# Attention and two MLPs on one core: input loads before weights, merged value sums, masks as matmuls, filler matmuls, a later third attention

## The chip, the cores and the metric

One core of a Trainium2 chip runs the whole program in one launch. The metric is the device time of an execution in microseconds (us); the time of a kernel is the median of its runs. The engines are PE (matmuls; PEld is its weight load), DVE (vector), ACT (scalar, activations), POOL (GpSimd) and SP, whose queue issues the loads and stores.

## What is computed

Four batches of eight heads, 576 positions, 64 channels; two attentions are added, and two MLPs follow on all 2304 tokens. From the reference, shortened:

```python
q_d = q.reshape(B, H, Sd, factor, D).mean(axis=3)     # factor 4, k and v alike
out_d = sm_attn(q_d, k_d, v_d)
out_up = np.repeat(out_d, factor, axis=2)
mask = np.abs(pos[:, None] - pos[None, :]) < factor
scores = np.where(mask, scale * np.matmul(q, k.transpose(0, 1, 3, 2)), -1000000000.0)
...
x = out_up + out_local                                 # 2304 x 512
h = x @ w_in
y = (h * np.cos(h)) @ moe_w_out                        # 512 -> 2048 -> 512
z = ((y @ w_a) * (y @ w_b)) @ moe2_w_out               # 512 -> 1536 -> 512
```

All of it is float32.

## The kernel before

The tokens are worked on in eight half-batches of 288 (`u` = 0 to 7; even `u` is the first half of a batch). Attention goes by pairs of heads (`hp` = 0 to 3). For each pair: `down_sums` adds groups of four keys (`kd`) and queries (`qd`), line L180 on DVE or L182 to L184 on POOL; `local_scores` multiplies five windows of 64 keys (L207, 10 matmuls of 64x64 that the profile shows as 20), adds the band mask on DVE (L218), takes the row maximum (L222) and subtracts it (L223); `down_scores` does the pooled scores (L234 to L237). Exponentials, normalisation, transposes through PE (L300, L309), the products with the values (L319, L326) and `combine` follow. `sum_vs` adds the four parts of the pooled values on POOL (L173 to L175). `xsplit_hi` and `xsplit_lo` split the result into a rounded high part (`xh`) and a low rest (`xl`).

Every weight chunk (128x512, 8 bytes an element as it lies in memory) is loaded (`wload`, L102) and made into a high and a low half by five instructions: L111 on ACT, L112 and L113 on DVE, L115 on ACT, L116 on POOL. There are 32 of them for the first MLP. A product is three matmuls (`mm3`, L429 to L431): high times high, high times low, low times high.

The first half-batch is done by itself (the prologue: lines 516 to 556). Then a loop over steps `g` runs one `h_mm` (12 matmuls into a PSUM tile `h`), the cosine (L475, L476, L480, L483, L484), the split of the result (L488, L492) and, three steps later, `back_mm` (12 matmuls into four `acc` tiles). Blocks 0 and 1 are the first two half-batches with the first 8 of 16 chunks, whose results go to `y_part`; half-batch 2 enters at step 32. The attention of the next half-batches is spread over the steps by `unit_slots(u, g0, gl)`: it begins at step `g0` and takes `gl` steps, by the table `C['T']`. For half-batch 2 that is `unit_slots(2, C["G2"], 2 * NF - C["G2"])`, from step 14 to 32.

The code is traced by a scheduler (Tile), which sets each engine's fixed order from its own estimates; each engine then runs its order and waits for semaphores. Loads and stores stand in SP's queue in order. PSUM has eight banks: `att` 2, `h` 2, `acc0` to `acc3`; in the prologue `att_ps` also takes those of `h` and `acc`. `vs` has one buffer for `u` > 0, `q` three, and the tiles of stores (`ev`) share three with `xf`.

Of the kernel before, what the change touches and what calls it, by code (L numbers as in the profile page):

```python
# [40 lines left out]
C = {'AHEAD': 8, 'LEAD': 4, 'NPRE': 4, 'ND': 'ddd', 'XL': 'dpp', 'SUMS0': 'dddd', 'SUMS1': 'pppp', 'GLO': 8, 'FS': 8, 'S1': 0.7, 'G2': 14, 'LC': 0, 'DM': 2, 'LAG': 3, 'NGS': 3, 'MK': 0, 'SB': 'ddd', 'NL': 'dpp', 'W0': 0, 'W1': 0, 'W2': 0, 'W3': 0, 'NWV': 3, 'NGH': 4, 'XB': 8, 'YE': 6, 'CA': 2, 'NR': 3, 'PA': 1, 'LAG2': 2, 'PK': 1.0, 'GE': 'ad', 'NXF': 3, 'LP': 0, 'T': {'sums': [0, 0.5, 1.0, 3.0], 'ls': [0, 0, 0, 1.5], 'ds': [1, 1.5, 3, 4], 'ex': 6, 'ln': [6.0, 9.5], 'dn': [6, 7, 9, 10], 'dt': [7, 9.5, 11, 12], 'lt': [7.5, 8.5, 12.0, 13.5], 'at': [9.5, 9.5, 13.5, 14.5], 'xh': [11.0, 12.0, 15.0, 15.5], 'xl': [12.5, 13.5, 15.5, 15.5]}, 'T1': {'sums': [0, 0, 1.0, 2.0], 'ls': [0.5, 1.5, 2.5, 3.5], 'ds': [1, 1.5, 3, 4], 'ex': 5, 'ln': [5.5, 8], 'dn': [5.0, 6.0, 8.0, 9.0], 'dt': [6.0, 7.5, 10.0, 11.0], 'lt': [7.0, 8.0, 12.0, 12.0], 'at': [9, 9, 13, 14], 'xh': [9.0, 10.0, 13.0, 14.0], 'xl': [9.5, 11, 15, 15]}}  # L41
# [16 lines left out]
def kernel(ctx, tc, qT, kT, vw, vds, w_in, w_out, w_a, w_b, w_out2, out):  # L58
# [96 lines left out]
    def load_vs(u, hp, par):  # L155
        b, half = divmod(u, 2)
        if half == 0:
            if u == 0:
                t = wp.tile([QD, 2, 4, D], F32, tag="w", name="vs0", bufs=33)
            else:  # L160
                t = at.tile([QD, 2, 4, D], F32, tag="vs", name="vs", bufs=1)
            ins = sp.dma_start(out=t, in_=vds[b, 2 * hp + par])
            after(ins, gate.get(u))
            vst[u, hp, par] = t

    def sum_vs(u, hp, par):
        b, half = divmod(u, 2)
        if half == 0:
            t = vst.pop((u, hp, par))
            if par == 0:  # L170
                vdt[b, hp] = at.tile([QD, 2, 2, D], F32, tag="vd", name="vd", bufs=4)
            o = vdt[b, hp][:, par]
# [25 lines left out]
    def local_scores(u, hp):  # L198
# [5 lines left out]
        for w, (off, _, _, _) in enumerate(window_cols(half)):  # L204
            for a in range(2):
# [5 lines left out]
                    start=not pem, stop=True,  # L211
# [293 lines left out]
    if C["MK"]:  # L505
        identb = const.tile([128, 128], BF16, name="identb")
        maskb = const.tile([128, W], BF16, name="maskb")
        pool.tensor_copy(out=identb, in_=ident)
        pool.tensor_copy(out=maskb, in_=mask)

    if C["W0"]:
        first.remove("acc3")
        wz = at.tile([128, 128], BF16, name="wz")
        dve.memset(wz, 0.0)
        wps = [ps.tile([128, 4, 128], F32, tag="acc3", name="wps")]
# [191 lines left out]
```

## Time and profile before

| | |
|---|---|
| median of three runs | 1035.38 us (1032.7, 1035.38, 1037.63) |
| the profiled execution | 1032.1 us, of which 1030.3 from its first to its last instruction (span) |
| busy: PE, PEld, DVE, ACT, POOL | 990.4, 901.4, 526.0, 470.0, 185.7 us |
| loads and stores | 72.70 MB, mean 71 GB/s |

PE's busy share counts matmuls that overlap one another; equal matmuls stand at two paces in this trace (rows 3), so a stretch with a full PE need not be PE at its fastest. A group's mean is over all its places; where a row gives the idle time before it and what ended it, that is a wait as the profile infers it. In a timeline "x12" means that twelve neighbours were merged, and the time is that from the first one's start to the last one's end.

### The profile page before, as it was taken

To read this page: it belongs to the slowest core of one execution; us is meant where nothing else is said; L and a number is where in the kernel's file an instruction comes from. 1 tells how busy PE (TensorE), PEld (TensorE's weight loads), DVE (VectorE), ACT (ScalarE), POOL (GpSimd) and SP (SyncE) were. 2 spreads that over 40 slices of the span, in tenths; PEclk is the share of its full clock that TensorE was granted. 3 is DMA by queue.
4 is the path that set the end of the run, shared out by engine and by line. 5 is a ranking of instruction groups with operands and counts; after the bars stand their busy time and mean duration, and the time that the engine had idled before them with its cause. 6 is when DMAs were issued, how large, how long until landed. Compare 5 with 4: busy or idle time off the path is not lost.

```text
span 1030.3 us, 16803 instructions
## 1 busy us (share of the span) xinstructions
PE 990.4 (96%) x6720; PEld 901.4 (87%) x6720; DVE 526.0 (51%) x1076; ACT 470.0 (46%) x1018; POOL 185.7 (18%) x215
## 2 busy tenths in 40 slices
PE   5978799999999899999999999999999999999998
PEld 4768799998989799899999988898898899889987
DVE  7889975676667465563687883121122113112111
ACT  4687676474747375564777653121122112111111
POOL 4878731012101300000232441000000001000000
PEclk9989999999999899999999999999999999999999
DMA  9645311312120201000443760020021002001000
GB/s 303 216 160 212 113 52 38 89 42 62 48 84 21 82 13 33 24 1 8 162 148 122 226 194 28 1 74 1 1 65 40 1 1 83 1 1 37 1 1 37
DMA packets 35021, 72.70 MB, mean 71 GB/s; under 512 B 5504, under 2 KB 19840, under 8 KB 34944
## 3 DMA queue, kind: packets, MB, share of 16 engines
q1 hardware_dynamic: 34944, 71.65, 21.8%
q8 instruction: 52, 0.85, 0.4%
q14 instruction: 25, 0.20, 0.1%
HBM read 61.01 MB, written 10.62 MB: 70 GB/s over the span
## 4 chain that ended last, share of the span: by engine, by line
PE 73%; issue 7%; POOL 7%; DVE 6%; DMA 5%; ACT 3%; SPq 0%; POOLq 0%; DVEq 0%
PE acc L429 9%; PE acc L430 9%; PE acc L431 9%; PE h L429 5%; PE h L431 5%; PE h L430 5%; PE pb L431 4%; PE pa L430 4%; PE pb L429 4%; PE pa L431 4%; PE pa L429 4%; PE pb L430 4%; POOL w L116 3%; DVE raw L113 2%; DMA vs<-in_vds_dram 2%
## 5 line engine op out<-in xcount | busy, mean ns | idle before, releaser
L429 PE MATMUL acc<-gh,w 128*128 128x288 f32 (+3 forms) x648 | 220.7, 341 | 1.1 <-DVE ev L468 1.1
L430 PE MATMUL acc<-gl,w 128*128 128x288 f32 (+3 forms) x648 | 217.5, 336 | 1.7 <-POOL gl L492 1.7
L431 PE MATMUL acc<-gh,w 128*128 128x288 f32 (+3 forms) x648 | 216.0, 333 | 0.0
L647 DVE TENSOR_TENSOR gs<-gs,pb 128x460 f32<-128x460 f32 (+1 forms) x60 | 38.0, 633 | 267.6 <-PE pb L431 267.5
L488 ACT ACTIVATE gh<-gs 128x288 fp32r<-128x288 f32 (+3 forms) x172 | 88.6, 515 | 161.8 <-DVE gs L647 119.2
L429 PE MATMUL h<-xh,w 128*128 128x288 f32 (+1 forms) x448 | 145.7, 325 | 6.0 <-DVE gs L484 6.0
L431 PE MATMUL h<-xh,w 128*128 128x288 f32 (+1 forms) x448 | 141.8, 317 | 1.7 <-POOL w L116 1.7
L430 PE MATMUL h<-xl,w 128*128 128x288 f32 (+1 forms) x448 | 141.7, 316 | 0.0
L492 DVE TENSOR_TENSOR gl<-gs,gh 128x288 fp32r<-128x288 f32 (+3 forms) x164 | 105.4, 643 | 62.1 <-ACT gh L488 60.9
L429 PEld LDWEIGHTS acc<-gh,w 128*128 128x128 f32 x648 | 122.9, 190 | 11.2 <-issue 3.5
L430 PEld LDWEIGHTS acc<-gl,w 128*128 128x128 f32 x648 | 123.1, 190 | 8.5 <-POOL gl L492 1.9
L431 PEld LDWEIGHTS acc<-gh,w 128*128 128x128 f32 x648 | 123.0, 190 | 5.8 <-issue 0.4
L644 ACT COPY gs<-pa 128x460 f32<-128x460 f32 (+1 forms) x60 | 32.5, 541 | 179.6 <-PE pa L431 179.6
L116 POOL TENSOR_TENSOR w<-raw,w 128x512 fp32r<-128x512 f32 x62 | 85.9, 1393 | 71.0 <-ACT w L115 70.9
L429 PEld LDWEIGHTS h<-xh,w 128*128 128x128 f32 x448 | 85.5, 191 | 11.8 <-DVE gs L484 8.9
L431 PEld LDWEIGHTS h<-xh,w 128*128 128x128 f32 x448 | 85.5, 191 | 3.5 <-POOL w L116 2.3
L430 PEld LDWEIGHTS h<-xl,w 128*128 128x128 f32 x448 | 85.5, 191 | 1.5 <-issue 0.6
L475 ACT ACTIVATE gs<-h 128x288 int32<-128x288 f32 (+1 forms) x112 | 49.5, 442 | 68.6 <-PE h L431 68.4
L476 DVE SCALAR_TENSOR_TENSOR gs<-gs,h 128x288 f32<-128x288 int32 (+1 forms) x112 | 55.1, 492 | 39.1 <-ACT gs L475 38.6
L429 PE MATMUL pa<-xh,w 128*128 128x460 f32 (+1 forms) x200 | 73.8, 369 | 1.1 <-ACT gs L644 1.1
L431 PE MATMUL pb<-xh,w 128*128 128x460 f32 (+1 forms) x200 | 74.4, 372 | 0.0
L430 PE MATMUL pa<-xl,w 128*128 128x460 f32 (+1 forms) x200 | 74.4, 372 | 0.0
(100 smaller groups left out, 1683.6 us busy)
## 6 DMA issues: line engine op xcount, KB each, us to landing
raw<-in_w_out_dram SPq DMA_DIRECT2D x28, 512.0 KB
raw<-in_w_in_dram SPq DMA_DIRECT2D x16, 512.0 KB
raw<-in_w_a_dram SPq DMA_DIRECT2D x12, 512.0 KB
raw<-in_w_b_dram SPq DMA_DIRECT2D x12, 512.0 KB
v<-in_vw_dram SPq DMA_DIRECT2D x16, 320.0 KB
q<-in_qT_dram SPq DMA_DIRECT2D x32, 146.0 KB
k<-in_kT_dram SPq DMA_DIRECT2D x16, 288.0 KB
vs<-in_vds_dram SPq DMA_DIRECT2D x32, 144.0 KB
```

The costliest lines, as they stand in the source:

```text
L113: ins = dve.scalar_tensor_tensor(out=lw, in0=hh, scalar=3, in1=lw, op0=ALU.logical_shift_left, op1=ALU.bitwise_or)
L116: lo_eng.tensor_tensor(out=t[:, 1], in0=lw.bitcast(F32), in1=t[:, 0].bitcast(F32), op=ALU.subtract)
L429: i = pe.matmul(ps_out, lh, rh, start=start, stop=False)
L430: pe.matmul(ps_out, lh, rl, start=False, stop=False)
L431: pe.matmul(ps_out, ll, rh, start=False, stop=stop)
L475: act.activation(out=k, in_=hps[g], func=AF.Copy, scale=1.0 / (2.0 * math.pi))
L476: dve.scalar_tensor_tensor(out=gs[g], in0=k, scalar=-2.0 * math.pi, in1=hps[g], op0=ALU.mult, op1=ALU.add)
L488: act.activation(out=gh[g], in_=gs[g], func=AF.Copy)
L492: eng.tensor_tensor(out=gl[g], in0=gs.pop(g), in1=gh[g].bitcast(F32), op=ALU.subtract)
L644: act.copy(out=gs[g], in_=pa)
L647: dve.tensor_tensor(out=gs[g], in0=gs[g], in1=pb, op=ALU.mult)
```

## The change

- The prologue's loads: SP issues the four `k` first and ACT's queue the four `q`; then one weight chunk, two `vs`, a weight, and values and `vs` by turns; the other weights last.
- For the first half-batch, the pooled values of a pair come by one load of 72x1024 in place of two of 72x512, and three adds of 72x256 replace six of 72x128. The layout of `vds` in memory is changed to suit.
- Pairs 2 and 3 of the first half-batch form `kd` and `qd` on POOL (`SUMS0` 'ddpp').
- For half-batches 0, 1 and 2 (`MK` 3) the mask is added by PE: a bf16 matmul of the identity with the mask, into the tile that the scores are then added to. The bf16 operands are the upper halves of the float32 identity and mask. DVE takes the maximum from PSUM and subtracts from PSUM.
- Filler matmuls of 128x512 in bf16, whose result nobody reads: 4 before the first scores, 3 after each of the four pairs' scores, 10 before the first transposes. They take the `acc3` bank in the prologue and are kept in program order.
- `local_scores` is written ahead of `down_sums` in the prologue.
- The third attention (half-batch 2) begins at step 18 in place of 14 (`G2`).

Its core as a diff:

```diff
-C = {... 'SUMS0': 'dddd', ... 'G2': 14, ... 'MK': 0, ... 'W0': 0, 'W1': 0, 'W2': 0, 'W3': 0, ...}
+C = {... 'SUMS0': 'ddpp', ... 'G2': 18, ... 'MK': 3, ... 'W0': 4, 'W1': 3, 'W2': 10, ...}
-                t = wp.tile([QD, 2, 4, D], F32, tag="w", name="vs0", bufs=33)
+                t = wp.tile([QD, 4, 4, D], F32, tag="w", name="vs0", bufs=33)
+                sp.dma_start(out=t, in_=vds[b, hp])
-            o = vdt[b, hp][:, par]
+            o = vdt[b, hp] if u == 0 else vdt[b, hp][:, 2 * par:2 * par + 2]
-                    start=not pem, stop=True,
+                    start=not pem, stop=not pem or w == NW - 1,
-                pe.matmul(wps[0], wz, wz.unsqueeze(1).to_broadcast([128, 4, 128]), start=True, stop=True)
+                tc.keep_in_program_order(pe.matmul(wps, identb, identb.unsqueeze(1).to_broadcast([128, 4, 128]), start=True, stop=True))
+    identb, maskb = (t.bitcast(BF16).rearrange("p (c t) -> p t c", t=2)[:, 1] for t in (ident, mask))
         for hp in range(HP):
             load_k(0, hp)
-            load_q(0, hp)
-            if hp < C["NPRE"]:
-                load_next(None)
-        for hp in range(HP):
-            for par in range(2):
-                load_vs(0, hp, par)
-        load_v(0)
-        for _ in range(C["AHEAD"] - C["NPRE"]):
+            load_q(0, hp, act)
+        load_next(None)
+        load_vs(0, 0, 0)
+        load_vs(0, 1, 0)
+        load_next(None)
+        load_v(0, 0)
+        load_vs(0, 2, 0)
+        load_vs(0, 3, 0)
+        load_v(0, 1)
+        for _ in range(C["AHEAD"] - 2):
             load_next(None)
         warm(C["W0"])
         for hp in range(HP):
+            local_scores(0, hp)
             down_sums(0, hp)
-            local_scores(0, hp)
             warm(C["W1"])
...
         down_exp(0, 3)
+        warm(C["W2"])
         for hp in range(HP):
-            for par in range(2):
-                sum_vs(0, hp, par)
+            sum_vs(0, hp, 0)
```

What the scheduler makes of it. PE's order at the start of the program, before (`att` is a score tile, `wps` the fillers' tile):

```order
L207 MATMUL att<-k,q 64x64 x10
L234 MATMUL att<-kd,qd 72x144
L207 MATMUL att<-k,q 64x64 x10
L234 MATMUL att<-kd,qd 72x144 x3
L207 MATMUL att<-k,q 64x64 x10
```

and now, where the numbers show which pair it is (`kd_183` and `qd_185` are pair 1, `k_97` and `q_99` pair 0):

```order
L235 MATMUL att_237<-kd_183,qd_185 72x144
L235 MATMUL att_238<-kd_183,qd_185 72x144
L390 LDWEIGHTS ident_75
L390 MATMUL wps_96<-ident_75 128x512
...
L390 MATMUL wps_96<-ident_75 128x512
L204 LDWEIGHTS ident_75
L204 MATMUL att_145<-mask_76,ident_75 128x320
L208 MATMUL att_145<-k_97,q_99 64x64 x10
```

PE's first matmuls are now the pooled scores of pair 1; four fillers and the mask stand ahead of the first local scores.

DVE's order at the start, before:

```order
L180 TENSOR_REDUCE kd<-k 128x144
L180 TENSOR_REDUCE qd<-q 128x72
L236 TENSOR_REDUCE mxd<-att 72x1
L112 TENSOR_SCALAR raw<-raw 128x512
L180 TENSOR_REDUCE kd<-k 128x144
L180 TENSOR_REDUCE qd<-q 128x72
L113 SCALAR_TENSOR_TENSOR raw<-raw 128x512
```

and now:

```order
L181 TENSOR_REDUCE qd<-q 128x72
L181 TENSOR_REDUCE kd<-k 128x144
L181 TENSOR_REDUCE qd<-q 128x72
L181 TENSOR_REDUCE kd<-k 128x144
L112 TENSOR_SCALAR raw<-raw 128x512
L113 SCALAR_TENSOR_TENSOR raw<-raw 128x512
L223 TENSOR_REDUCE mx<-att 128x5
L224 TENSOR_TENSOR smx<-att,mx 128x5x64
```

The sums of pairs 0 and 1 stand together, and the first weight's two instructions stand ahead of the first row maximum.

SP's order around the third attention, before (`vs` are the pooled values of half-batch 2, `y_part` the stores of a block's result):

```order
L162 DMA vs<-in_vds_dram 72x512 x2
L143 DMA q<-in_qT_dram 128x292 x2
L162 DMA vs<-in_vds_dram 72x512 x2
L143 DMA q<-in_qT_dram 128x292
L162 DMA vs<-in_vds_dram 72x512 x2
L143 DMA q<-in_qT_dram 128x292
L162 DMA vs<-in_vds_dram 72x512
L470 DMA y_part<-ev 128x288 x4
```

and now:

```order
L102 DMA raw<-in_w_out_dram 128x512
L163 DMA vs<-in_vds_dram 72x512 x6
L143 DMA q<-in_qT_dram 128x292 x2
L471 DMA y_part<-ev 128x288 x4
L143 DMA q<-in_qT_dram 128x292 x2
```

Six `vs` loads in a row now stand ahead of the `q` loads.

## Rows read from the trace of the kernel before

**Rows 1.** Table of stretches: length, busy PE, PEld, DVE, ACT, POOL, PE clock, DMA.

```profile
3.68:36.77 33.09, 24.74 (x244) 19.74 (x244) 27.03 (x67) 17.55 (x51) 19.32 (x29) 1.00 0.87 303
36.77:118.23 81.46, 66.23 (x584) 58.26 (x583) 74.83 (x134) 63.42 (x152) 65.57 (x59) 0.92 0.55 183
118.23:160.00 41.77, 38.89 (x305) 36.48 (x306) 33.68 (x82) 28.90 (x66) 17.49 (x22) 0.96 0.15 43
160.00:220.00 60.00, 60.00 (x586) 56.44 (x585) 37.43 (x95) 36.54 (x89) 3.22 (x4) 1.00 0.20 62
0.00:34.42 34.42, 22.39 (x235) 17.39 (x235) 24.69 (x62) 16.97 (x48) 18.80 (x37) 1.00 0.89 306
```

**Rows 2.** Chain of waits of the prologue: start us, us, what.

```profile
7.78 7.67 DMA vs<-in_vds_dram
...
31.99 0.45 POOL vd L175
```

**Rows 3.** Timeline of PE and its weight loads around the first `h`: start, us.

```profile
34.42 0.61 PE L429 MATMUL h<-xh,w 128*128 128x288 f32 x1
34.58 0.33 PEld L430 LDWEIGHTS h<-xl,w 128*128 128x128 f32 x1
...
37.23 0.44 PE L431 MATMUL h<-xh,w 128*128 128x288 f32 x1
...
40.77 0.29 PE L429 MATMUL h<-xh,w 128*128 128x288 f32 x1
...
41.43 0.29 PE L431 MATMUL h<-xh,w 128*128 128x288 f32 x1
```

**Rows 4.** Timeline of DVE, the fifteenth `h`.

```profile
118.23 0.45 DVE L476 SCALAR_TENSOR_TENSOR gs<-gs,h 128x288 f32<-128x288 int32 x1 [0.51 <-ACT gs L475]
```

**Rows 5.** DVE's groups by shape, 0 to 140 us: busy us, mean ns, idle before.

```profile
L223 DVE TENSOR_TENSOR smx<-smx,mx 128x320 f32<-128x320 f32 x12 | 8.0, 681 | 0.0
L180 DVE TENSOR_REDUCE kd<-k 128x144 f32<-128x576 f32 x8 | 5.9, 742 | 4.0 <-DMA k<-in_kT_dram 4.0
L218 DVE TENSOR_TENSOR smx<-att,mask 128x320 f32<-128x320 f32 x12 | 5.6, 479 | 0.6 <-PE att L207 0.6
L180 DVE TENSOR_REDUCE qd<-q 128x72 f32<-128x288 f32 x9 | 4.0, 439 | 0.0
```

**Rows 6.** The same for 0 to 36.77 us.

```profile
L223 DVE TENSOR_TENSOR smx<-smx,mx 128x320 f32<-128x320 f32 x4 | 1.8, 480 | 0.0
```

**Rows 7.** POOL's groups by shape, 2.4 to 34.15 us.

```profile
L175 POOL TENSOR_TENSOR vd<-vd,vs 72x128 f32<-72x128 f32 x8 | 6.4, 801 | 0.6
L173 POOL TENSOR_TENSOR vd<-vs 72x128 f32<-72x128 f32 x8 | 5.6, 704 | 13.2 <-DMA vs<-in_vds_dram 13.2
L174 POOL TENSOR_TENSOR vd<-vd,vs 72x128 f32<-72x128 f32 x8 | 3.8, 476 | 0.6
L116 POOL TENSOR_TENSOR w<-raw,w 128x512 fp32r<-128x512 f32 x1 | 1.3, 1302 | 0.4 <-ACT w L115 0.4
```

**Rows 8.** Timeline of DVE and ACT, the first two weights.

```profile
6.62 0.43 DVE L112 TENSOR_SCALAR raw<-raw 128x512 uint32<-128x512 uint32 x1
...
9.08 0.66 ACT L111 ACTIVATE raw<-raw 128x512 f32<-128x512 f32 x1 [1.29 <-DMA raw<-in_w_in_dram]
```

**Rows 9.** Timeline of PE at the third attention's first scores.

```profile
120.04 1.33 PE L207 MATMUL att<-k,q 64*64 64x64 f32 x20 [2.58 <-DVE smx L218]
...
121.71 0.44 PE L430 MATMUL acc<-gl,w 128*128 128x288 f32 x1
121.95 0.44 PE L431 MATMUL acc<-gh,w 128*128 128x288 f32 x1
```

**Rows 10.** Chain of waits, 340 to 358 us.

```profile
341.52 2.36 DMA vs<-in_vds_dram
...
345.95 4.12 DMA y_dram<-ev
```

**Rows 11.** Timeline of PE, 347 to 355 us.

```profile
350.71 0.80 PE L207 MATMUL att<-k,q 64*64 64x64 f32 x20 [2.04 <-DVE xf L338]
...
354.25 1.33 PE L207 MATMUL att<-k,q 64*64 64x64 f32 x20 [2.41 <-DVE smx L218]
```

More of the change, by code (lines that the diff above doesn't have):

```diff
@@ L134, in load_k, with load_q @@
             kt[b, hp] = t
-    def load_q(u, hp):
+    def load_q(u, hp, eng=sp):
         if u < NU:
@@ L142, in load_q, with load_v @@
                 t = at.tile([128, HALF], F32, tag="q", name="q", bufs=3)
-            sp.dma_start(out=t, in_=qT[b, hp, :, BASE[half]:BASE[half] + HALF])
+            eng.dma_start(out=t, in_=qT[b, hp, :, BASE[half]:BASE[half] + HALF])
             qt[u, hp] = t
-    def load_v(u):
-        for pr in range(HP // 2 if u < NU else 0):
+    def load_v(u, *prs):
+        for pr in (prs or range(HP // 2)) if u < NU else ():
             if u == 0:
@@ L158, in load_vs @@
             if u == 0:
-                t = wp.tile([QD, 2, 4, D], F32, tag="w", name="vs0", bufs=33)
+                t = wp.tile([QD, 4, 4, D], F32, tag="w", name="vs0", bufs=33)
+                sp.dma_start(out=t, in_=vds[b, hp])
             else:
                 t = at.tile([QD, 2, 4, D], F32, tag="vs", name="vs", bufs=1)
-            ins = sp.dma_start(out=t, in_=vds[b, 2 * hp + par])
-            after(ins, gate.get(u))
+                ins = sp.dma_start(out=t, in_=vds[b, hp, :, 2 * par:2 * par + 2])
+                after(ins, gate.get(u))
             vst[u, hp, par] = t
@@ L170, in sum_vs @@
             if par == 0:
[L171 to L172 removed]
+                vdt[b, hp] = at.tile([QD, 4, D], F32, tag="vd", name="vd", bufs=4)
+            o = vdt[b, hp] if u == 0 else vdt[b, hp][:, 2 * par:2 * par + 2]
             pool.tensor_tensor(out=o, in0=t[:, :, 0], in1=t[:, :, 1], op=ALU.add)
@@ L319, in attend @@
                 pe.matmul(
-                    p[64 * a:64 * a + 64, NB:NB + QD], vdt[b, hp][:, a, c], pd[u, hp][:, 2 * a + c],
+                    p[64 * a:64 * a + 64, NB:NB + QD], vdt[b, hp][:, 2 * a + c], pd[u, hp][:, 2 * a + c],
                     start=(c == 0), stop=(c == 1),
@@ L503 @@
                            fill=-8e9, base=3, channel_multiplier=-1)
[L505 to L515, printed above, removed]
+    identb, maskb = (t.bitcast(BF16).rearrange("p (c t) -> p t c", t=2)[:, 1] for t in (ident, mask))
+    first.remove("acc3")
+    wps = ps.tile([128, 4, 128], F32, tag="acc3", name="wps")
     if True:
@@ L676, in _layout @@
                 vw[u, hp // 2, hp % 2, :, w] = v[b, 2 * hp:2 * hp + 2, s0:s0 + W].transpose(1, 0, 2)
-    vds = v.reshape(B, H, 2, QD, 4, D).transpose(0, 1, 3, 2, 4, 5)
+    vds = v.reshape(B, HP, 2, 2, QD, 4, D).transpose(0, 1, 4, 2, 3, 5, 6).reshape(B, HP, QD, 4, 4, D)
     return {
```

4 lines of the change are left out of this document (1 added, 3 removed).

## The prediction

> **What bounds the kernel now.** The page comes first, but its shares of busy time are averages over stages. The table of stretches says where PE is not full [rows 1]. From 160 us PE is busy 60.00 of 60.00, and there the diff changes nothing but an address. Before 160 us three stretches differ. From 3.68 us, where DVE gets its first input, to 36.77, where DVE writes the last low half of the first half-batch, DVE is busy 27.03 of 33.09 us and PE 24.74. From there to 118.23, DVE is busy 74.83 of 81.46 and PE 66.23. From 118.23 to 160, PE is busy 38.89 of 41.77 and DVE only 33.68. So up to 118 us the engine nearest to full is DVE, after it PE. The chain of waits names another engine for the prologue: the 24 adds of `sum_vs` on POOL, which start when the first `vs` lands at 15.45 and end at 32.44 [rows 2], with the first weight's low half behind them and the first `h` matmul at 34.42 [rows 3]. Both readings hold: POOL ended last, and DVE had only 6.06 us to spare. That decides the size of my number, because the change takes much from POOL and little from DVE.
>
> **The change, part by part.** I count up to 118.23 us on DVE, where the fifteenth `h` is reduced (L476, the fifteenth of its line, [rows 4]), and after it on PE.
>
> *Masks as matmuls.* Twelve L218 adds go, 479 ns each [rows 5]. Eight of them stand before 118.23: 8 x 0.479 = 3.8 us off DVE. The last four, of the third half-batch, lie where DVE has slack and count nothing here. PE gets twelve matmuls of 320 columns. No row shows one in bf16; twelve of 288 columns start within 2.81 us in the first `h` group, 0.24 apart after the first, and 0.13 apart later [rows 3], so 0.15 to 0.27 each. Eight lie beside DVE's work while PE is idle for 8 and 15 us of the two stretches: nothing. Four lie where PE is full: up to 1.1 us, and I take 0.6. If the cover goes, all twelve cost 3.2.
>
> *The subtraction reads PSUM.* L223 has both inputs in SBUF and takes 480 ns in the prologue (4 of them) and 681 on average over twelve, so (12 x 681 - 4 x 480) / 8 = 782 for the other eight [rows 5, 6]. L218, which reads PSUM, stays at 479 in all. The new subtraction has L218's kind of input, and I price it like L218: 0.30 us off each of the four in the second half-batch, 1.2 us (between 0 and 1.2). The Trainium skill's "SBUF — State Buffer", section "Who interferes with whom", gives a reason: a DVE instruction with two SBUF inputs contends with a GpSimd instruction that reads SBUF, one with a single SBUF input does not; by it the whole 1.2 comes. Its "Perfetto Trace Analysis", section "Optimizing Scalar/DVE Operations", speaks against the edit, with about 125 ns of access overhead on PSUM against 60 on SBUF; an estimate from that page is 16 reads x 65 ns = 1.0 us more, and the sum would be 7.4 in place of 8.4. The rows do not show that: 479 with a PSUM input, 480 without.
>
> *Pooled sums.* The `kd` and `qd` reductions of pairs 2 and 3 leave DVE: 2 x (0.742 + 0.439) = 2.4 us [rows 5].
>
> *POOL.* The 24 adds of 72x128 took 5.6, 3.8 and 6.4 us by line, 15.8 together [rows 7]. Twelve of 72x256 replace them. The nearest rows are 72x128 at its shortest, 0.45 [rows 2], and 128x512 at 1.30 (L116, rows 7); four times the width costs 0.85 more, so 256 costs some 0.73: 8.8 us in all. Twelve small adds for `kd` and `qd` come to POOL, about 0.5 each by L174's 476 ns: 6 us. POOL can start them when pairs 2 and 3 land, near 8.7, not at 15.6, and is done by some 25 us. POOL no longer ends the prologue. DVE's instructions with two SBUF inputs meet as many POOL adds as before.
>
> *Loads.* Keys and weights of before shared one queue. The tiles hold 288 (`k`), 146 (`q`), 512 (a weight) and 144 KB (`vs`). In their old order 946 KB are in at 6.62 us, when DVE starts on the first weight, 1892 at 9.08, when ACT starts on the second [rows 8], and 3928 at 15.45 [rows 2]. Now the four pairs (1736 KB) are first: by the same rate they are in at 8.7, and the first weight, at 2248 KB, at 10.2 instead of 6.62. ACT issues the four `q` loads before its first work, which needs PE's first scores: nothing. DVE's queue is now both sums of pairs 0 and 1, then the first weight's two instructions, and only then the first row maximum. So DVE works some 2.4 us on the sums, waits for pair 1 (about 2 us) and for the weight until 10.2 (about 2), then for ACT's 0.66 us in between [rows 8]: near 5 us idle by 11.6. The waits that follow (local scores behind fillers, the last `qd` from POOL, the attends) I put at 3. DVE idles 8 in place of 6.06: 2.0 us lost. The bounds are 5 (a gain of 1) and 10 (a loss of 4). On that path DVE's last low half of the first half-batch comes at 3.7 + 24.3 + 8 = 36 us, hardly earlier than 36.77; 24.3 is 27.03 less 4.3 (four masks, 2.4 of sums), plus 1.6 for one weight chunk and one maximum that now stand ahead of it.
>
> *Fillers.* 26 matmuls of 512 columns cost 26 x 0.24 = 6.1 us at the later rate and 26 x 0.43 = 11.1 at the first. The column of the granted clock reads 1.00 in the prologue, but the first `h` group stands 0.24 apart, the rate of the lower of the two levels (1.2 GHz), after a prologue in which PE paused often; 0.13 is reached only after 40 us [rows 3]. With fillers the attention of the prologue and the first group may run at 2.4 GHz. I count neither gain nor cost, since DVE covers it: PE had 12 us idle before 34.42 [rows 1].
>
> *Third attention later.* Its scores now start after the last weight has been split on DVE. Of the 41.77 us after 118.23 PE loses 2.88 idle [rows 1], and some 1.1 to slow matmuls after the 2.58 us wait at 117.4 (six `acc` at 0.24, the first of them in [rows 9], and twenty L207 in 1.33 instead of 0.80, [rows 9, 11]). The third of the new `L208` groups can still wait for a PSUM buffer. I take 4.0 less 0.4 for that and less the 0.6 of masks: 3.0, between 0 and 4.
>
> **Sum:** 3.8 + 1.2 + 2.4 - 2.0 + 3.0 = 8.4 us less. The profiled execution took 1032.1 (span 1030.3 and 1.8 around it), so 1023.7; the median of the three runs stands 3.3 above it, and for a median I forecast **1027.0**. With both ends of every unknown it is 1021 to 1034.
>
> **Rivals.**
> 1. *POOL alone ended the prologue.* If DVE's waits in the new order are as short as before or shorter, the first `h` matmul comes with POOL's end plus one L116, near 27 us, 7.4 earlier, and twelve matmuls at 0.13 for 0.24 give 1.3: 8.7 in place of the prologue's share of my sum (1.9 + 2.4 - 2.0 = 2.3). Gain 14.8: 1020.6. For it speaks the chain; against it 27.03 of 33.09. Chance 0.22.
> 2. *The loads of `vs` block the queue.* In SP's new order six `vs` loads in a row, each waiting for one buffer, stand ahead of a `q` and four stores of the first partial result. The same pattern stands in the trace at 341 to 354: `vs`, then the `y_dram` stores [rows 10], then DVE, and PE waits 2.04 and 2.41 us [rows 11] and its twenty L207 take 1.33 instead of 0.80; with the `acc` matmuls after them, slow as in [rows 9], some 6 us in all. At the third attention that eats 6 of the 8.4: gain 2.4, 1033.0. Against it: the weights are through by then and the POOL queue is short. Chance 0.15.
> 3. *Scores held longer in PSUM.* A score buffer is freed by the subtraction, not the mask add, so one maximum (0.47) later. Before, PE already waited for L218 in front of L207. If each of the eight scores of half-batches two and three pays it, 3.8 us: gain 4.6, 1030.8. Chance 0.14.
> 4. *The fillers are the path: slower.* All 26 stand in PE's queue before the first transposes, the first four behind the sums of pair 1 (near 8 us). If their weight loads do not hide (0.33 us beside 0.43 at the low clock, [rows 3] for the load), a filler costs 0.76 and all cost 19.8. PE's 22.39 us before 34.42 [rows 1] plus these plus 1.1 of masks, from 8 us on, end at 51: the first `h` is 17 us late, or 8 if the loads hide fully. In the middle 12.8 late, less 6.1 of the other terms that survive: 1042. It decides from fillers more than 0.6 us apart, or a first `h` after 36 us. Against it: the diff's fillers share one weight matrix, and later loads hide. Chance 0.05.
>
> **How the numbers follow.** My forecast has 0.42; 0.02 is left for a gain beyond rival 1. A measurement of this kernel can tell about 0.5%, 5.2 us, from no change: faster means below 1030.2. Six in seven of my own case lie there, all of rival 1 and the rest, and some 0.4 of rival 3: 0.36 + 0.22 + 0.02 + 0.06 = 0.66. Rival 2, most of rival 3 and the tail of my case are 0.27 within. Slower has rival 4 and some mishap of rival 2: 0.07. For 8 in 10 the range takes in rivals 1 to 3 and leaves out rival 4: 1019 to 1036.
>
> **What would show it.** In the new profile: no DVE mask adds on the first twelve score tiles; the PSUM subtraction at 0.48 throughout; POOL's value sums done by 25 us; DVE idle near 8 us before the last low half; PE with less than 0.5 us of waits between the fifteenth L476 and 160 us; an unchanged wait near 341 to 354, moved earlier by the gain. A first `h` at 27 us makes rival 1 right, after 36 rival 4; a wait behind `vs` in SP's queue near 115 to 135 us rival 2. If DVE has more than 10 us idle up to the first L476, my term for the loads is wrong.

## The result, and the profile after

| | before | changed |
|---|---|---|
| median | 1036.51 us (1032.70 to 1038.73, 4 runs) | 1048.01 us (1045.04 to 1050.09, 4 runs) |
| ratio | 1 | 1.0113, 95% interval 1.0072 to 1.0153 |
| the profiled execution, its span | 1032.1, 1030.3 us | 1048.62, 1046.8 us |

The change makes the kernel 1.1% slower. The forecast was 1027.0 (1019 to 1036) with 0.07 for slower: wrong in sign, and outside the range. Of the runs below, two of the eight executions of e3 (2489.96 us, the profiled one, and 1908.6) and one of the four of e13 (5355.39) were disturbed and are left out of every number.

The page after the change: span, busy time of PE and DVE in 40 slices, and the granted clock.

```profile
span 1046.8 us, 16853 instructions
...
PE 1010.5 (97%) x6758; PEld 912.2 (87%) x6758; DVE 521.6 (50%) x1060; ACT 469.4 (45%) x1018; POOL 180.3 (17%) x215
...
PE   6988789999999999999999999999999999999998
...
PEclk9559999999999989999999999999999999999999
```

DVE works 4.4 us less than before (526.0), as intended, and PE 20.1 us more (990.4). The second and third digit of the clock stand at 5. The two profiled executions lie further apart (16.5 us) than the medians (11.5), so the sums below are those of one execution each.

**A ledger of PE at equal work.** After its last `h` of the first MLP is reduced, the changed kernel stays 16.2 us behind (L477 last starts at 580.8, L476 of before at 564.6), so I set 0 to 398.00 before against 0 to 414.20 after. First the table of stretches of before, then that of after (columns as in [rows 1]).

```profile
0.00:398.00 398.00, 363.41 (x3446) 331.80 (x3448) 287.34 (x685) 253.50 (x618) 130.01 (x171) 0.97 0.31 100
```

```profile
0.00:414.20 414.20, 383.52 (x3482) 342.64 (x3484) 282.94 (x669) 253.12 (x618) 124.07 (x171) 0.92 0.30 96
```

PE's groups in the same two stretches, before and after (busy us, mean ns, idle before).

```profile
L429 PE MATMUL h<-xh,w 128*128 128x288 f32 x316 | 97.9, 310 | 6.0 <-DVE gs L484 6.0
L429 PE MATMUL acc<-gh,w 128*128 128x288 f32 x300 | 94.0, 313 | 1.1 <-DVE ev L468 1.1
```

```profile
L430 PE MATMUL h<-xh,w 128*128 128x288 f32 x316 | 102.1, 323 | 12.7 <-DVE gs L485 12.7
L430 PE MATMUL acc<-gh,w 128*128 128x288 f32 x300 | 94.9, 316 | 0.1
...
L390 PE MATMUL wps<-ident 128*128 128x512 bf16 x26 | 7.7, 426 | 0.0
L204 PE MATMUL att<-mask,ident 128*128 128x320 bf16 x12 | 4.4, 370 | 2.0 <-DVE smx L224 2.0
```

316 and 300 on both sides: the same work. PE's idle time is 34.59 us before (398.00 less 363.41) and 30.68 after, 3.9 less. Its busy time is 20.1 more. From the start of each to the start of the next instruction the fillers take 6.9 of that and the masks 3.6; the other 9.6 is the same matmuls running slower. The matmuls that both have are busy for 65.3 us at 1.2 GHz after the change and for 45.0 before; with `h` matmuls 0.24 apart at that level and 0.13 at the other, the 20.3 more are worth some 9 us (an estimate), so nearly all of the 9.6 is the clock. 20.1 less 3.9 is the 16.2.

**Where along the way.** The stages between the k-th reductions of `h` (starts of L476 or L477), us:

| kernel | to the 1st | 1st to 5th | 5th to 15th | 15th to 28th | 28th to last |
|---|---|---|---|---|---|
| before | 38.47 | 34.07 | 45.69 | 54.17 | 392.17 |
| changed | 42.68 | 40.26 | 48.07 | 58.64 | 391.11 |

The first stage holds the prologue, the second the second attention, the fourth the third attention. All of the loss arises in the first 190 us.

**The clock.** The table of stretches after the change, cut where the granted clock changes (0.50 is 1.2 GHz, 1.00 is 2.4).

```profile
10.40:24.10 13.70, 11.45 (x116) 6.15 (x112) 12.78 (x35) 8.02 (x32) 12.40 (x18) 1.00 1.01 350
24.10:44.50 20.40, 20.40 (x174) 16.08 (x173) 12.10 (x28) 11.24 (x26) 8.49 (x11) 0.50 0.55 198
44.50:48.00 3.50, 1.88 (x35) 1.35 (x36) 2.55 (x4) 2.79 (x7) 3.06 (x4) 0.99 0.17 45
48.00:68.40 20.40, 19.98 (x95) 15.34 (x91) 13.11 (x31) 12.40 (x33) 7.80 (x9) 0.50 0.59 202
68.40:71.90 3.50, 1.15 (x9) 0.83 (x9) 3.50 (x14) 2.48 (x11) 3.08 (x3) 0.99 0.00 0
71.90:82.10 10.20, 8.66 (x81) 7.65 (x80) 9.08 (x18) 6.74 (x17) 5.91 (x6) 0.50 0.32 110
```

PE's timeline of the same stretch.

```profile
7.16 1.89 PE L390 MATMUL wps<-ident 128*128 128x512 bf16 x4
...
18.30 2.44 PE L390 MATMUL wps<-ident 128*128 128x512 bf16 x10
...
23.15 0.63 PE L301 MATMUL att<-ident,smx 128*128 128x128 f32 x4 [0.92 <-ACT smd L312]
...
24.96 1.32 PE L327 MATMUL att<-smx,v 64*64 64x60 f32 x20
...
31.59 0.59 PE L430 MATMUL h<-xh,w 128*128 128x288 f32 x1
...
33.51 1.32 PE L327 MATMUL att<-smx,v 64*64 64x60 f32 x20
...
36.77 0.91 PE L208 MATMUL att<-k,q 64*64 64x64 f32 x12
...
50.62 0.45 PE L430 MATMUL h<-xh,w 128*128 128x288 f32 x1
50.86 0.45 PE L431 MATMUL h<-xl,w 128*128 128x288 f32 x1
...
70.37 0.55 PE L301 MATMUL att<-ident,smx 128*128 128x128 f32 x3 [2.00 <-POOL smx L279]
```

The first fillers raise the clock at 10.4: four take 1.69 us, 0.42 apart, ten later 2.28, 0.23 apart. From 20.6 to 24.1 PE pauses 1.6 us among the transposes, and the clock falls. From 24.1 to 44.5 PE is busy all the time, and from 48.0 to 68.4 for 19.98 of 20.40 us, and in both the clock stays at 0.50: `h` matmuls stand 0.24 apart. It rises, PE pauses (1.62 us at 45.7, 2.00 at 68.4), and it falls again. A second profiled execution of the same kernel (e9) shows the same: 1.2 GHz from 24.6 to 41.7, 48.5 to 65.6 and 69.0 to 82.6. Before, the matmuls ran at 1.2 GHz up to 37.8 us (the profile records no level until the first change, and prints 1.00 there), then from 61.7 to 71.9, and twice briefly up to 123. For the same reason the "17 us at 0.50" that the expectations give for before leaves out its first 37.8 us, and a mean granted clock is compared here within one kernel, or between two whose first record stands at about the same place.

So in the new order PE is the path from 24 us on: in the chain of waits it is PE's own attends and `h` matmuls, at 1.2 GHz, from 23.96 to 45.45 without another engine. What stands in that chain was also reordered by the scheduler. Before, the twelve matmuls of the first `h` stand together from 34.42, and it is reduced at 38.47. In the change six of them stand ahead of the second attention's first mask, with an attend among them, and the others among its scores: it starts at 31.59 and is reduced at 42.68. In the ledger this order is no cost of its own, since PE is busy all the while, but it makes the first `h` late.

### The profile page after: what moved, and what is told of

It is laid out like the page before. It is cut to its first block, busy times and chain, and to the rows that moved or that the text cites. A ratio compares the mean times of both kernels' runs of the same rounds, so it can differ in the third digit from the quotient of the medians.

```text
span 1046.8 us, 16853 instructions
## 1 busy us (share of the span) xinstructions
PE 1010.5 (97%) x6758; PEld 912.2 (87%) x6758; DVE 521.6 (50%) x1060; ACT 469.4 (45%) x1018; POOL 180.3 (17%) x215
## 4 chain that ended last, share of the span: by engine, by line
PE 80%; DVE 8%; POOL 4%; ACT 3%; issue 3%; DMA 3%; SPq 0%; POOLq 0%; DVEq 0%
PE acc L430 10%; PE acc L431 10%; PE acc L432 10%; PE h L430 6%; PE h L431 6%; PE h L432 5%; PE pb L432 4%; PE pa L431 4%; PE pb L430 4%; PE pa L432 4%; PE pa L430 4%; PE pb L431 4%; DVE raw L113 2%; POOL w L116 2%; PE att L327 2%
## 5 line engine op out<-in xcount | busy, mean ns | idle before, releaser
L430 PE MATMUL h<-xh,w 128*128 128x288 f32 (+1 forms) x448 | 149.9, 335 | 12.7 <-DVE gs L485 12.7
L431 PE MATMUL h<-xl,w 128*128 128x288 f32 (+1 forms) x448 | 145.1, 324 | 0.0
L432 PE MATMUL h<-xh,w 128*128 128x288 f32 (+1 forms) x448 | 144.1, 322 | 0.0
L430 PEld LDWEIGHTS acc<-gh,w 128*128 128x128 f32 x648 | 124.2, 192 | 9.9 <-issue 3.3
L432 PEld LDWEIGHTS acc<-gh,w 128*128 128x128 f32 x648 | 124.2, 192 | 6.5 <-issue 1.1
L430 PEld LDWEIGHTS h<-xh,w 128*128 128x128 f32 x448 | 88.0, 196 | 20.3 <-DVE gs L485 16.1
L431 PEld LDWEIGHTS h<-xl,w 128*128 128x128 f32 x448 | 88.1, 197 | 2.3 <-issue 1.1
L432 PEld LDWEIGHTS h<-xh,w 128*128 128x128 f32 x448 | 88.0, 196 | 1.7 <-issue 0.4
L476 ACT ACTIVATE gs<-h 128x288 int32<-128x288 f32 (+1 forms) x112 | 49.4, 441 | 73.5 <-PE h L432 73.4
L477 DVE SCALAR_TENSOR_TENSOR gs<-gs,h 128x288 f32<-128x288 int32 (+1 forms) x112 | 55.1, 492 | 43.7 <-ACT gs L476 43.3
L485 DVE SCALAR_TENSOR_TENSOR gs<-gs,h 128x288 f32<-128x288 f32 (+1 forms) x112 | 55.0, 491 | 43.7 <-ACT gs L484 42.7
```

Of the source, the lines that this page charges most:

```text
L430: i = pe.matmul(ps_out, lh, rh, start=start, stop=False)
L431: pe.matmul(ps_out, lh, rl, start=False, stop=False)
L432: pe.matmul(ps_out, ll, rh, start=False, stop=stop)
L476: act.activation(out=k, in_=hps[g], func=AF.Copy, scale=1.0 / (2.0 * math.pi))
L477: dve.scalar_tensor_tensor(out=gs[g], in0=k, scalar=-2.0 * math.pi, in1=hps[g], op0=ALU.mult, op1=ALU.add)
L485: dve.scalar_tensor_tensor(out=s, in0=s, scalar=1.0, in1=hps[g], op0=ALU.subtract, op1=ALU.mult, reverse0=True)
```

## The experiments

All times are against the kernel before on the same chip; its median there was 1033.8 to 1034.5 us. Every version is ordered anew by the scheduler, so an edit can also move instructions that it does not name. By the names in the traces, masks and fillers left out, e2 has four of PE's 6720 matmuls at another place than before and nothing moved on DVE, e7 and e12 nothing moved up to 115 and 106 us; but e6 has some 150 matmuls and 160 of DVE's 1044 instructions moved, e5 some 450 and 180, and e1 against the change some 130 and 150. Where orders differ, the difference of two runs is not the price of the edit alone. Theories: 1, the fillers and the clock; 2, the new order; 3, scores held longer; 4, PE pays for what is put on it, since its idle time comes from chains of waits and not from a busy DVE; 5, the clock in the prologue; 6, attention as PE's filling work.

| run | what it is | median us | ratio to before (95%) |
|---|---|---|---|
| e1 | change, no fillers | 1041.82 | 1.0067 (1.0048 to 1.0086) |
| e2 | before, with the 26 fillers | 1033.49 | 0.9997 (0.9983 to 1.0011) |
| e3 | change, masks on DVE | 1038.9 | 1.0049 (1.0033 to 1.0065) |
| e4 | change, last ten fillers off | 1042.72 | 1.0073 (1.0051 to 1.0096) |
| e5 | before, masks as matmuls | 1039.38 | 1.0057 (1.0039 to 1.0075) |
| e6 | before, masks left out | 1036.31 | 1.0031 (1.0017 to 1.0046) |
| e7 | before, third attention later | 1040.62 | 1.0064 (1.0042 to 1.0086) |
| e8 | order, merged and pooled sums alone | 1036.36 | 1.0027 (1.0006 to 1.0049) |
| e9 | the change again | 1047.65 | 1.0113 (1.0067 to 1.0159) |
| e10 | change, 8 more fillers | 1041.86 | 1.0074 (1.0055 to 1.0092) |
| e11 | e8 with fillers and the 8 more | 1031.43 | 0.9980 (0.9967 to 0.9993) |
| e12 | before, third attention earlier | 1038.99 | 1.0045 (1.0028 to 1.0061) |
| e13 | e10, third attention back | 1039.6 | 1.0062 (1.0040 to 1.0083) |
| e14 | e11, 14 more fillers | 1035.94 | 1.0021 (1.0009 to 1.0033) |
| e15 | e10, masks on DVE | 1040.44 | 1.0072 (1.0046 to 1.0099) |
| e16 | e7, stores by ACT | 1040.95 | 1.0070 (1.0049 to 1.0091) |

### Fillers: e1, e2, e4

e1 drops `wps` and sets `W0`, `W1`, `W2` to 0; e4 sets `W2` to 0. e2 gives the kernel before the `warm` of the change and

```diff
-'W0': 0, 'W1': 0, 'W2': 0
+'W0': 4, 'W1': 3, 'W2': 10
         down_exp(0, 3)
+        warm(C["W2"])
```

> The changed kernel without its 26 fillers; all else stays. Theory 1 (fillers and clock): the fillers raise TensorE's clock to 2.4 GHz at 10 us, the pauses among the transposes drop it at 24 us, and after a drop that follows fillers it stays at 1.2 GHz for tens of us although PE is busy. Then without fillers the trace has at most some 20 us at a granted clock of 0.50 in the first 90 us (17 before, 51 after), and the time is 1024 to 1033, 15 to 24 below the change. Theory 2 (new order): the pauses of the new prologue drop the clock with or without fillers; then 40 to 50 us at 0.50 and 1043 to 1050. Theory 3 (scores held longer in PSUM, masks): DVE's later release makes PE wait; no fillers change nothing of it: 1043 to 1050, with the 12 us of waits of the h matmuls for DVE's gs still there.

> The kernel before with nothing added but the same 26 fillers at the same places of its prologue (4 ahead of the first pair, 3 after each pair's scores, 10 ahead of the value sums). Theory 1: slower than before by 8 to 17 us (1045 to 1053), with 35 to 55 us at 0.50 in the first 90 us. Theories 2 and 3: 1034 to 1040, the clock of before (some 17 us at 0.50).

> The changed kernel without the last ten fillers (those ahead of the first transposes); the first sixteen stay. Theory 1 in the form that the drop from 2.4 GHz is what costs: the clock is still raised at 10 us by the first sixteen, drops earlier, at 18 to 21, and comes back earlier by as much at most: 1040 to 1048, 40 us or more at 0.50. If only a full stretch just ahead of the pause does the harm, 1024 to 1033 with some 20 us at 0.50. Theories 2 and 3: 1043 to 1050.

None came out as one theory had it. Without fillers the change is still 0.67% above before, so the fillers are not the whole cause. The clock has a part without them too: e1's six executions run from 1044.46 us at a mean granted clock of 0.968 to 1038.59 at 0.979. With fillers it is 1.13%, some 0.46% or 4.8 us more, though the two intervals overlap and the orders differ as well. In the old order, which they leave as it was, they cost nothing (e2): in its profiled execution PE is busy 4.3 us more up to the same last `h` (367.75 of 400.30), about half of that out of its idle time, and the medians are equal. e4 lies close to e1, which points to the last ten, though the intervals are too wide to show it. The clock of its profiled execution was at 1.2 GHz from 21.4 to 45.3 all the same, so that part of theory 1, a drop that only comes after a full stretch, falls.

### Masks: e3, e5, e6

e5 sets `MK` to 3 in the kernel before, with the bf16 views of the change. e6 is e5 without the matmul; e3 sets `MK` to 0 in the change.

```diff
-                    start=not pem, stop=True,
+                    start=not pem, stop=not pem or w == NW - 1,
```

> The kernel before with one part of the change alone: the masks of the first three half-batches as twelve matmuls, the subtraction reading PSUM. The prediction's term: DVE bounds the stretch up to 118 us and gets rid of eight adds and 1.2 us of shared access, so 1029 to 1031 (5 below before). Theory 4 (PE pays): PE idles where it waits for a chain of steps, not for a busy DVE, so freed DVE time gives nothing, and each added matmul (0.30 us in the run of the change, twelve are 3.6) is paid in full: 1036 to 1039. Theory 3 (scores held longer): 1037 to 1040, with more waits of PE for DVE's subtraction.

> The kernel before with no mask at all on the first twelve score tiles: neither the add on DVE nor a matmul, and the subtraction reads PSUM (the masking of these three half-batches is left out of the result). If DVE bounds the stretch up to 118 us: 1029 to 1031. If freed DVE time gives nothing: 1032 to 1036, within 0.2% of before. The difference from the run with the masks as matmuls is the price of twelve matmuls on PE: 0 if they are hidden, 3.6 if they are all paid.

> The changed kernel with the mask added on DVE again in all half-batches and no mask matmuls; fillers and order stay. Theory 3: the waits of PE for DVE's subtraction and for gs shrink from some 17 us to 8, and the time is 1036 to 1041. Theory 1: the clock is as long at 0.50 as in the change (45 to 55 us), DVE has 3.8 us more work: 1046 to 1053. Theory 2: the same.

e5, by itself, costs 0.57%, where the prediction had a gain of 5 us; e6 removes the adds at no price on PE and still gains nothing. This is the most direct test of "DVE bounds". The table of stretches of e6 up to the same last `h`:

```profile
0.00:400.90 400.90, 366.88 (x3442) 335.08 (x3444) 278.84 (x673) 254.10 (x618) 124.64 (x171) 0.97 0.31 99
```

DVE is busy 8.5 us less than before and PE's idle time is 34.02 for 34.59. PE's busy time is 3.5 more with no matmul added: in this execution the clock rose at 47.3 us in place of 37.8. Why the time of e6 is 2.5 us above before in ten executions, and not equal, was not shown; its moved orders are one candidate. e5's twelve matmuls take 3.5 us from start to next start, and e5 less e6 is 3.1. That fits theory 4, paid and not hidden, but does not show it: e5's nine executions run from 1042.70 us at a mean granted clock of 0.966 to 1036.27 at 0.979, the last no slower than e6's 1036.31, so the clock, or the order, can be behind the difference as well. In the profiled one, that of 1036.27, most of the loss arises in the fourth stage, 58.10 for 54.17. In e3 DVE adds the masks again beside the fillers, and the time is 0.64% lower than the change's; theory 3 had 1036 to 1041 for it, but no trace of it shows the waits.

### The third attention: e7, e12, e16

```diff
-'G2': 14
+'G2': 18
```

(12 in e12); e16 adds to e7

```diff
-                sp.dma_start(out=dst[:, m, s0:s0 + k], in_=t[:, o:o + k])
+                (act if dst is y_part else sp).dma_start(out=dst[:, m, s0:s0 + k], in_=t[:, o:o + k])
```

> The kernel before with the third attention 4 steps later and nothing else. The prediction's term: 3.0 us less, 1031. Theory 4: the waits move with the attention, and its chain (scores, maximum, exponential, sums, transposes) is paid again at the later place: within 3 us of before on either side, 1033 to 1037. The run without fillers points to 2 to 3 us more, for it took 49.3 us from the fourteenth to the twenty-fifth h where the kernel before took 46.7.

> The kernel before with the third attention 2 steps earlier and nothing else. Theory 6: its matmuls are what PE does while the weights are still split on DVE, ACT and POOL; four steps later PE was idle there (6.6 us more) and had the work to do later. Two steps earlier fills more of that idle time: 1027 to 1032. Rival: DVE is busy 38 of 40 us there and is what the attention then waits for: 1034 to 1041.

> The kernel before with the third attention 4 steps later (1040.6) and the stores of the first partial result issued by ACT instead of SP, so that they are not stuck behind the six value loads. If rival 2 of the prediction is the price: DVE's wait of 3.6 us for the old ev buffer and PE's 2.3 behind it go, and the time is 1034 to 1037. If the price is PE's idle time while weights are split and the attention's work paid in full later: 1039 to 1042.

e7 is the cleanest of all: up to the fifteenth `h` it keeps a lead of 0.8 us, then the stage to the 28th takes 62.09 in place of 54.17. PE's idle time in that stage is 7.67 us in place of 2.88, and its busy time 54.42 in place of 51.29, at a granted clock of 0.92 in place of 0.97. The table of stretches of before, then that of e7:

```profile
118.23:172.40 54.17, 51.29 (x440) 48.47 (x441) 39.69 (x96) 36.88 (x86) 19.10 (x24) 0.97 0.16 48
```

```profile
117.40:179.49 62.09, 54.42 (x462) 49.65 (x461) 40.77 (x95) 35.72 (x85) 18.86 (x24) 0.92 0.14 44
```

What PE then waits for shows in the change too. Its timelines of POOL, ACT, DVE and PE (one fence, in that order):

```profile
130.50 0.91 POOL L174 TENSOR_TENSOR vd<-vs 72x128 f32<-72x128 f32 x1
...
132.22 0.80 POOL L176 TENSOR_TENSOR vd<-vd,vs 72x128 f32<-72x128 f32 x1
132.97 1.29 POOL L116 TENSOR_TENSOR w<-raw,w 128x512 fp32r<-128x512 f32 x1
...
134.30 0.66 ACT L115 ACTIVATE w<-raw 128x512 fp32r<-128x512 f32 x1 [2.15 <-POOL w L116]
134.86 0.43 ACT L484 ACTIVATE gs<-gs 128x288 f32<-128x288 f32 x1
...
135.32 0.45 DVE L485 SCALAR_TENSOR_TENSOR gs<-gs,h 128x288 f32<-128x288 f32 x1 [2.63 <-ACT gs L484]
...
135.83 0.40 PE L430 MATMUL h<-xh,w 128*128 128x288 f32 x1 [2.36 <-DVE gs L485]
```

POOL does the value sums of half-batch 2 between the last weights. ACT's queue stands at L115 for the weight, the cosine (L484) stands behind it, DVE behind that, and PE's next `h` behind DVE. Before, PE worked on the third attention's scores at such times; now it has none, and the same scores come when PE is full. Theory 6 fits "later". It does not fit "earlier": e12 costs 0.45% too, in the range of its rival. In its trace PE does 49 matmuls more between the fifth and the fifteenth `h`, but its idle time there does not shrink (7.77 us for 7.30), and in the stage to the 28th it has 41 fewer and idles 6.43 in place of 2.88. Another 3.7 us of that trace are lost up to the fifth `h`, where the order is still that of before and the clock fell at 46.3, so they are not the edit's.

Rival 2 of the prediction is tested by e16. In the change SP stands at the six `vs` for 27.58 us, and the stores come behind them; in e7 DVE waits for that. SP's timeline of the change, then DVE's of e7, then a row of e16's waits (us in total, times, longest):

```profile
119.63 27.58 SPq L163 DMA_DIRECT2D vs<-in_vds_dram  x6
...
148.83 3.59 SPq L471 DMA_DIRECT2D y_part<-ev  x4
```

```profile
142.47 0.46 DVE L468 COPY ev<-acc 128x288 f32<-128x288 f32 x1 [3.62 <-DMA y_part<-ev]
```

```profile
DVE ev L468 <- DMA y_part<-ev: 1.0, 2, 0.5
```

The queue was blocked as rival 2 had it, and taking the stores off it takes most of DVE's wait away; the time stays at 1040.95. So rival 2 is not the price of 6.8 us; with four executions each, some 2 us of it could still be in there.

### The order alone: e8

The change with `W0` to `W2` 0, `MK` 0, `G2` 14.

> The changed kernel without fillers, with the masks on DVE again and the third attention where it was: what is left is the new order of loads, the merged value sums, two pairs' sums on POOL and the scores issued ahead of the sums. The prediction's terms: 2.4 less 2.0, so 1033 to 1034; its first rival (POOL alone ended the prologue): 1024 to 1027. Theory 2 (the new order itself costs): 1037 to 1041. By the run without fillers (8 us above before) less 3.6 for the masks and 0 to 3 for the attention: 1035 to 1038.

0.27% above before, between the prediction's 1033 to 1034 and theory 2. Its stages: 40.36, 34.57, 46.01, 53.65, 392.35. The prologue with everything earlier on POOL ends 1.9 us later. Its first `h` matmul starts at 34.80 (34.42 before): from 23.81 on the chain is PE's transposes, attends and `h` matmuls (0.69 us of ACT among them), at 1.2 GHz up to 37.8. Here moving loads and POOL forward did not end it sooner, and three of the first `h`'s matmuls stand behind the second attention's first scores.

### Holding the clock: e9, e10, e11, e14

```diff
                 local_transpose(0, hp // 2, 1)
+                warm(4 if hp == 0 else 0)
             down_transpose(0, hp)
+            warm(4 if hp == 0 else 0)
             attend(0, hp)
```

e11 adds `MK` 0 and `G2` 14; e14 has `W2` 16 and 12 for the first 4.

> The change itself once more, beside the following three on one chip, for the price of its fillers and for how much its time varies: 1043 to 1049, 1.0 to 1.4% above before.

> The change with eight more fillers in the pauses of the first two groups of transposes (four behind the local, four behind the downsampled of the first pair). Theory 5: in the new order PE itself is the path from 24 us on, and it runs at 1.2 GHz from 24.1 to 44.5 because it paused from 21.3 to 24. With the pauses filled the clock stays at 2.4 GHz: an attention's twenty matmuls take 0.80 for 1.33, the first h is reduced (first L477) at 33 to 37 instead of 42.7, and the time is 1034 to 1041, 6 to 10 below the change. Rival: the clock drops all the same, or what follows waits for DVE and weights anyway: 1042 to 1050.

> The new order, merged sums and fillers with the same eight more, but the masks on DVE and the third attention where they were before. Theories 4 and 5 together: the run of the order alone (1036.4) less 6 to 10 for the clock held through the first attention: 1026 to 1031, below before. If the fillers and the clock are no gain: 1035 to 1041.

> The new order with masks on DVE and the third attention where they were before, with 16 fillers ahead of the first transposes and 12 and 4 among them (10, 4 and 4 in the run before, where pauses of 1.3 and 1.8 us were left and the clock dropped at 22.7 in the profiled execution). If the clock now stays at 2.4 GHz from 10 us to the second attention: 1025 to 1030. If the added fillers delay the transposes as much as the clock gives: 1030 to 1034.

e10's table of stretches and PE's timeline:

```profile
10.80:31.20 20.40, 18.71 (x245) 11.77 (x244) 19.01 (x50) 14.40 (x48) 13.90 (x20) 1.00 1.01 344
31.20:34.70 3.50, 3.50 (x26) 2.70 (x26) 3.50 (x7) 2.17 (x5) 2.95 (x5) 0.51 0.40 158
```

```profile
24.18 0.79 PE L327 MATMUL att<-smx,v 64*64 64x60 f32 x20
...
30.83 0.40 PE L430 MATMUL h<-xh,w 128*128 128x288 f32 x1
```

With the pauses filled but for 0.4 to 0.9 us each, the clock stays up to 31.2, twenty attends take 0.79 for 1.32, the first L477 comes at 37.48 for 42.68, and the time falls by 5.8 us (1047.65 to 1041.86) though PE has eight fillers more. That is what theory 5 had; its size was at the edge of both expectations. e9 shows the same by chance, and more sharply, since it is one program in one order: three of its executions took 1046.05 to 1049.49 us at a mean granted clock of 0.967 to 0.973, one 1037.64 at 0.988. So the lower clock goes with 8.4 to 11.9 us of the change's time, and with the clock high it is still 3.2 above before.

e11 is the one version below before: 0.9980, an interval that leaves out 1, and 16.2 us below the change of e9. Its 0.2% is less than the half per cent that the prediction took as measurable, and is told by its twelve executions. In its profiled execution the clock was not held (1.2 GHz from 22.7 to 43.2, after pauses of 1.30 and 1.83 us), so what it gains by the clock is not shown there. But that execution, 1034.96 us, is one of the two slowest of the twelve (1034.96 and 1035.46, both at 0.980; the others 1029.75 to 1033.36 at 0.981 to 0.983), and e8, which lacks the fillers and has some 60 matmuls moved, stands at 0.968 to 0.975 in all of its seven and 4.9 us higher: that points to the clock. e14 filled those pauses, and held 2.4 GHz to 31.7: its first `h` starts at 31.54, 2.9 us earlier than before, but is reduced at 38.50 for 38.47, since the clock then fell, and the time is 0.4% above e11's. Starting the first `h` sooner was worth nothing there. What e11 gains by stays open.

### The square: e13, e15

`G2` 14, and `MK` 0, in e10.

> The run with the clock held (change plus eight fillers, 1041.9) with the third attention where it was before. If its later place costs 6.6 here as it did alone: 1034 to 1037. If the later place costs nothing here and the masks cost all ten: 1040 to 1043.

> The run with the clock held with the masks added on DVE again, the third attention in its later place. If the masks as matmuls cost 5.7 here as they did alone: 1035 to 1038. If they cost only their own 3.1 us on PE less what DVE gains: 1038 to 1041.

Neither part 1031.43, masks alone 1039.6, later attention alone 1040.44, both 1041.86. Each by itself costs 8 to 9 us beside the other parts, and the second adds next to nothing. For the later attention that is the attention's own price: the orders of e11 and e15 are the same up to 117 us. The orders of e11 and e13 differ from the start. The stages say where. With the masks on PE in the new order the fifth `h` is reduced at 75.5 to 76.8 us (e1 75.51, e4 76.33, e10 76.14, e13 76.79; 82.3 and 82.9 in e9 and the change, where the clock fell), without at 72.2 to 74.9 (e8 74.93, e11 73.43, e14 72.82, e15 72.20). With the later attention the fourth stage takes 58 to 64 (e10 58.55, e15 63.91), without mostly 53 to 56 (e11 53.48, e13 55.65, but e14 57.21, and e5 58.10 in the old order). Why the fourth stage is cheaper for a kernel that is already late in the second was not shown.

## Why the prediction was wrong, by its steps

1. **The bound** failed first. "Up to 118 us the engine nearest to full is DVE" is true as a share [rows 1] and was taken as a price list. The prediction counted every microsecond off DVE as one off the time. In e6 8.5 us of DVE's work went away, 0.6 us of PE's idle time, and nothing of the time (2.5 us more, with part of the orders moved).
2. **Masks off DVE, 3.8 us less**: 0.57% more by themselves (e5). "Eight lie beside DVE's work while PE is idle ...: nothing" did not come true; the twelve take 3.6 us of the ledger, 0.30 each. That this is the whole of e5's price is not shown.
3. **The subtraction, 1.2 less**: the duration was right, 482 ns for the twelve that read PSUM. The gain went elsewhere. Rows of DVE's groups, before (0 to 398.00), then after (0 to 414.20):

```profile
L113 DVE SCALAR_TENSOR_TENSOR raw<-raw 128x512 uint32<-128x512 uint32 x32 | 28.6, 900 | 1.4 <-ACT raw L111 1.3
L112 DVE TENSOR_SCALAR raw<-raw 128x512 uint32<-128x512 uint32 x32 | 22.5, 717 | 0.1
L223 DVE TENSOR_TENSOR smx<-smx,mx 128x320 f32<-128x320 f32 x28 | 15.8, 568 | 0.0
```

```profile
L113 DVE SCALAR_TENSOR_TENSOR raw<-raw 128x512 uint32<-128x512 uint32 x32 | 30.5, 961 | 1.2 <-ACT raw L111 0.9
L112 DVE TENSOR_SCALAR raw<-raw 128x512 uint32<-128x512 uint32 x32 | 26.5, 845 | 3.1 <-DMA raw<-in_w_in_dram 3.1
L224 DVE TENSOR_TENSOR smx<-smx,mx 128x320 f32<-128x320 f32 x16 | 8.0, 497 | 0.0
...
L224 DVE TENSOR_TENSOR smx<-att,mx 128x320 f32<-128x320 f32 x12 | 5.8, 482 | 0.1
```

   The 28 subtractions take 13.8 for 15.8 us, and L112 and L113 take 57.0 for 51.1 (55.4 in e5, 54.9 in e6). It looks as if the weight splits lose beside POOL what the subtraction no longer does; that is argued, not shown.
4. **Pooled sums and POOL**: right as durations (twelve adds of mostly 0.72 us, 0.73 predicted; POOL done at 23.6, by 25 predicted), and worth nothing, since PE ends the prologue.
5. **Loads, 2.0 more**: the text set its own test, "more than 10 us idle". DVE idles 12.2 us between its first input at 4.28 and the first L477 at 42.68 (26.21 busy of 38.40), 10.4 of it up to its last low half at 39.96: 3.13 waiting for the first weight at 9.54, and 2.55 behind scores that PE did at 1.2 GHz, among the first `h`'s matmuls. The term is wrong, by what it left out: PE.
6. **Fillers, neither gain nor cost**: right in the old order (e2), wrong in the new, where the change with them stands 0.46% above e1. "DVE covers it" looked at PE's idle time before 34.42; in the new order PE is the path from 24 us.
7. **Third attention later, 3.0 less**: 0.64% more by itself (e7), and 9.0 us more in e15 than in e11. The term priced the idle time at the old place after 118 us and not what the matmuls covered there.

The sum of the stated terms is right, but their stated bounds add up to 1023.0 to 1033.2, not 1021 to 1034.

Of the rivals, 1 fell: POOL was done at 23.6, and the first `h` started at 31.59, not at 27. Rival 2's block came true and was not the price (e16). Rival 3 fell: PE's waits for DVE's mask or subtraction (L219, L224) are 4.4 us after in the ledger's stretch, 5.4 for L218 before. Rival 4 had the sign and neither test of its mechanism: fillers stood at most 0.43 us apart, and the first `h` came before 36. The late wait [rows 11] is there once, 2.40 us at 369.87.

On the clock, the first `h` group "may run at 2.4 GHz" was left at that. What the clock cost, nearly all of the 9.6 us of PE's ledger, had no term: this is the largest single loss, and the prediction put it at nothing. The Trainium skill's "TensorE: Matmul & The Clock Gate", section "What's actually happening", says that the low level is the default and that activity releases it. The rise at 10.4 us behind the first fillers agrees; the stretch from 48.0 to 68.4 us, with PE busy 19.98 of 20.40 at 0.50, does not.

What stays open: why e6 is above before; why e12 costs; why masks and later attention do not add up; and how much of what masks and fillers cost is the order that the scheduler then made.

## What to carry to other kernels

An engine that is busy nine tenths of a stretch is not yet a price for its work. Leave some of that work out and see whether the idle time of the engine behind it shrinks, before paying for it with work on that engine. And ask of work that is to be moved away from a gap what will fill the gap then. Where a scheduler orders the engines anew for each version, compare the orders before you credit the edit with the difference.

## What was not expected of the hardware

- TensorE stayed at 1.2 GHz through 20.4 us of almost unbroken matmuls, twice, and in both profiled executions of the change for 17 us or more, after it had fallen behind pauses of 0.5 to 2 us. With most of the pauses among the first transposes filled it stayed at 2.4 GHz up to 31.2 (e10).
- L112, with one input, takes 0.41 us at its shortest. Two of them took 4.32 while POOL worked on without a gap. DVE's timeline after the change, then POOL's:

```profile
105.47 4.32 DVE L112 TENSOR_SCALAR raw<-raw 128x512 uint32<-128x512 uint32 x2
```

```profile
104.71 0.79 POOL L175 TENSOR_TENSOR vd<-vd,vs 72x128 f32<-72x128 f32 x1
105.58 0.62 POOL L176 TENSOR_TENSOR vd<-vd,vs 72x128 f32<-72x128 f32 x1
106.16 0.81 POOL L493 TENSOR_TENSOR gl<-gs,gh 128x288 fp32r<-128x288 f32 x1
106.93 2.57 POOL L116 TENSOR_TENSOR w<-raw,w 128x512 fp32r<-128x512 f32 x2
```

  The Trainium skill's "SBUF — State Buffer", section "Who interferes with whom", names `tensor_scalar` among the operations that can take the port pair shared with GpSimd when their operands allow it, and says that whoever issues first then holds the pair for the whole instruction. The rows agree that L112 loses beside POOL: up to 420 us the 19 that overlap a POOL instruction take 1.14 on average, the 13 others 0.42. The 3.99 of the longest reached over four POOL instructions; which mode L112 ran in no run shows.
